# A one-token attention and MLP mix: the output row's second half summed in a second column group of the TensorE array, and three weight loads cut differently

## The chip, the cores and the metric

The kernel runs on one core of one Trainium2 chip. The metric is the device time of the slowest (here: the only) core, in microseconds (us). Several executions are timed for each kernel, and one more is profiled. The span that a profile or a run lists for its core is about 1.8 us shorter than the time of that execution in most cases and repeats more closely, so I use both, and say which.

## The reference, cut to what matters

One token `x` (576 numbers) goes through two branches that are mixed by a gate: attention with 32 query heads over the last 4096 positions of a cache with 16 key/value heads, and a GELU MLP with 4608 hidden units.

```python
g = sigmoid((x * gate_w).sum(-1))
q = x @ wq                                   # 576 -> 32 heads x 128
o = softmax(q @ k.T / sqrt(128)) @ v         # last 4096 positions, 16 kv heads
a = o.reshape(4096) @ wo                     # 4096 -> 576
h = gelu(x @ w1 + b1)                        # 576 -> 4608
b = h @ w2 + b2                              # 4608 -> 576
y = g * a + (1 - g) * b
```

With one token there is almost no reuse: 53.6 MB of weights and cache are read, each byte is used once or twice, and every product is a matrix times one vector.

## The kernel before

All large transfers are issued in one queue in the order of use: w1, wq, eight K tiles, eight V tiles (with the first half of w2 among them), wo, and the second half of w2. The output row y is accumulated in PSUM (the memory that the matmuls write to) over the whole kernel. Its 576 fp32 columns are kept in two accumulators of 288, so each row of wo or w2 costs two matmuls with one stationary column:

```python
NH = D // 2                                            # 288
ya_ps = ps_y.tile([1, NH], FP32, name="ya_ps")
yb_ps = ps_y.tile([1, NH], FP32, name="yb_ps")

def y_add(vec, row, start=False, stop=False):
    nc.tensor.matmul(ya_ps[:], lhsT=vec, rhs=row[:, 0:NH], start=start, stop=stop, skip_group_check=True)
    nc.tensor.matmul(yb_ps[:], lhsT=vec, rhs=row[:, NH:D], start=start, stop=stop, skip_group_check=True)
```

The loads that the change touches, and the end of the kernel:

```python
for k in range(KM):                                    # KM = 4: w1 in four pieces
    nc.sync.dma_start(out=w1_m[:, k, :], in_=w1_src[:, k, :])
# ... (wq, K, softmax, V, first half of w2 cut)
for r in range(0, RO, 8):                              # RO = 32: wo in four pieces of 8 rows
    nc.sync.dma_start(out=wo_t[:, r : r + 8, :], in_=wo_src[:, r : r + 8, :])
for b, j0, j1 in [(1, 0, 9), (1, 9, 13), (1, 13, 16), (1, 16, NJ)]:   # NJ = 18 rows of w2
    load_w2(b, j0, j1)
# ... (scaling of o cut)
for r in range(RO):
    y_add(ov[:, r : r + 1], wo_t[:, r, :])
y_w2(1)                                                # 18 rows, y_add each

out_row = const.tile([1, D], BF16, name="out_row")
nc.vector.tensor_copy(out=out_row[:, 0:NH], in_=ya_ps[:])
nc.scalar.copy(out=out_row[:, NH:D], in_=yb_ps[:])
nc.sync.dma_start(out=out.rearrange("a b d -> (a b) d"), in_=out_row[:])
```

A "row" below is one `r` of wo or one `j` of w2: 128 partitions of 576 bf16 numbers, 147 KB, and two matmuls.

Of the kernel before, what the change touches and what calls it, by code (L numbers as in the profile page):

```python
# [8 lines left out]
FP32 = mybir.dt.float32  # L9
# [7 lines left out]
def kernel(  # L17
# [15 lines left out]
    nc = tc.nc  # L33

    P = 128
    D = 576
# [7 lines left out]
    NJ = FB // P  # L44
    NF = NB * NJ
    NPAIR = Hkv // 2
    KM = 4
# [9 lines left out]
    ps_y = ctx.enter_context(tc.tile_pool(name="ps_y", bufs=1, space=bass.MemoryType.PSUM))  # L57
# [15 lines left out]
    w1_m = w1_t[:, 0 : KM * F].rearrange("p (k n) -> p k n", k=KM)  # L73
    w1_l = w1_t[:, KM * F :]
    w1_src = B_w1[0:DM, :].rearrange("(p k) n -> p k n", k=KM)
    for k in range(KM):
        nc.sync.dma_start(out=w1_m[:, k, :], in_=w1_src[:, k, :])
    nc.sync.dma_start(out=w1_l, in_=B_w1[DM:D, :].rearrange("r (two n) -> (r two) n", two=2))

    wq_t = big.tile([P, KM * Hq * Dh + QH], BF16, name="wq_t", tag="A")  # L80
# [43 lines left out]
    for j in range(4):  # L124
        nc.vector.tensor_copy(
            out=perm[:, j], in_=idv[:, j // 2, :, j % 2].unsqueeze(1).to_broadcast([P, 4, 32])
# [9 lines left out]
    for t in range(2):  # L136
# [3 lines left out]
        lhsT=xd[:].rearrange("p a t -> p (a t)"),  # L140
        rhs=one_b[0:1, 0:2],
        start=True,
        stop=True,
# [9 lines left out]
        out=junk_row[:],  # L153
# [17 lines left out]
        out=omg[:], in0=g_t[:], scalar1=-1.0, scalar2=1.0, op0=ALU.mult, op1=ALU.add  # L171
# [3 lines left out]
        out=b2g[:], in0=b2_row[:], scalar1=omg[0:1, 0:1], scalar2=None, op0=ALU.mult  # L175
# [2 lines left out]

    NH = D // 2
    ya_ps = ps_y.tile([1, NH], FP32, name="ya_ps")  # L180
    yb_ps = ps_y.tile([1, NH], FP32, name="yb_ps")

    def y_add(vec, row, start=False, stop=False):
        nc.tensor.matmul(ya_ps[:], lhsT=vec, rhs=row[:, 0:NH], start=start, stop=stop, skip_group_check=True)  # L184
        nc.tensor.matmul(yb_ps[:], lhsT=vec, rhs=row[:, NH:D], start=start, stop=stop, skip_group_check=True)  # L185

    y_add(one_f[0:1, 0:1], b2g[0:1, :], start=True)


    h_ps = ps_s.tile([P, NF], FP32, name="h_ps", tag="s")  # L190
    for k in range(KM):
        for c in range(NF):
# [3 lines left out]
                lhsT=w1_m[:, k, f0 : (c // NJ + 1) * FB : NJ],  # L196
                rhs=xt[:, k : k + 1],
                start=(k == 0 and c == 0),
                stop=False,
                skip_group_check=True,  # L200
            )
    for j in range(NJ):
        nc.tensor.matmul(  # L203
            h_ps[:, j:NF:NJ],
            lhsT=w1_l[:, j:FB:NJ],
            rhs=xl[:, 0:2],
            start=False,
            stop=(j == NJ - 1),
            skip_group_check=True,
# [4 lines left out]
        out=hx[:], in0=h_ps[:], in1=b1_t[:].rearrange("p b j -> p (b j)"), op=ALU.add  # L214
# [4 lines left out]
        out=z2[:], in0=z2[:], scalar1=2.0 * C0 * 0.044715, scalar2=2.0 * C0, op0=ALU.mult, op1=ALU.add  # L219
# [8 lines left out]
        out=gt[:], in0=hx[:], scalar=omg[:, 0:1], in1=e_h[:], op0=ALU.mult, op1=ALU.mult  # L228
# [4 lines left out]
    for k in range(KM):  # L233
        for j in range(Hq):
            nc.tensor.matmul(  # L235
                q_ps[:, j : j + 1],
                lhsT=wq_m[:, k, j * Dh : (j + 1) * Dh],
                rhs=xt[:, k : k + 1],
                start=(k == 0 and j == 0),
                stop=False,  # L240
                skip_group_check=True,
            )
    for j in range(Hq // 2):
        nc.tensor.matmul(
            q_ps[:, j : Hq : Hq // 2],
            lhsT=wq_l[:, j * Dh : (j + 1) * Dh],
            rhs=xl[:, 0:2],
            start=False,
            stop=(j == Hq // 2 - 1),
            skip_group_check=True,  # L250
# [4 lines left out]
    for j in range(4):  # L255
        nc.tensor.matmul(
            qj_ps[:, j, :, :].rearrange("p i x -> p (i x)"),
            lhsT=perm[:, j, :, :].rearrange("p b l -> p (b l)"),
            rhs=q_b[:],
            start=True,  # L260
            stop=True,
        )
    for b in range(4):
# [4 lines left out]
            out=diag[:, :, 0:512].rearrange("p i (j m) -> p i j m", m=P)[:, :, :, 0:4],  # L268
            in_=qj_ps[rows].rearrange("p j i x -> p i j x"),
# [13 lines left out]
    for n in range(4):  # L283
        for e in range(2):
            nc.tensor.matmul(  # L285
                s_ps[:, n // 2, n % 2],
                lhsT=no_l[0:1, e, :],
                rhs=no_r[0:1, e, :],
                start=(e == 0),
                stop=False,  # L290
                skip_group_check=True,
            )
    for i in range(NPAIR):
        k_t = load_pair(A_k_cache, i)
        for c1 in range(2):
            kt = early[:, c1 * W : (c1 + 1) * W]
            nc.vector.transpose(  # L297
                out=kt.bitcast(FP32), in_=k_t[:, c1 * W : (c1 + 1) * W].bitcast(FP32)
            )
            kv = kt.rearrange("p (n c b k t) -> p n c b k t", n=2, b=2, k=32, t=2)  # L300
            for j in range(4):
                for n in range(2):
                    nc.tensor.matmul(  # L303
                        s_ps[:, c1, n],
                        lhsT=qz[:, i, j, :],
                        rhs=kv[:, n, :, j // 2, :, j % 2],
                        start=False,
                        stop=(i == NPAIR - 1 and j == 3),
                        skip_group_check=True,
# [4 lines left out]
    for c1 in range(2):  # L314
        nc.vector.reduce_max(
            out=m2[:, c1 : c1 + 1], in_=s_ps[:, c1].rearrange("p n k -> p (n k)"), axis=AX.X
# [19 lines left out]
    for c1 in range(2):  # L336
        nc.scalar.activation(  # L337
            out=p_x[:, c1 * 1024 : (c1 + 1) * 1024],
            in_=s_ps[:, c1].rearrange("p n k -> p (n k)"),
# [6 lines left out]
            out=pt[:, c1 * NCH : (c1 + 1) * NCH, :].rearrange("p c h -> p (c h)"),  # L346
            in_=p_x[:, c1 * 1024 : (c1 + 1) * 1024],
# [3 lines left out]
    for c1 in range(2):  # L351
        nc.vector.tensor_scalar(
            out=sl[:, c1, :], in0=lo32[:], scalar1=sums[:, c1 : c1 + 1], scalar2=None, op0=ALU.mult
# [8 lines left out]
    for a in range(4):  # L362
        nc.vector.tensor_scalar(
            out=rh[:, :, a], in0=rg[:], scalar1=hi4[:, a : a + 1], scalar2=None, op0=ALU.mult
# [7 lines left out]
    def load_w2(b, j0, j1):  # L372
        nc.sync.dma_start(out=w2_t[:, b, j0:j1, :], in_=w2_src[:, b, j0:j1, :])

    def y_w2(b, j0=0, j1=NJ):
        for j in range(j0, j1):
            y_add(gt[:, b * NJ + j : b * NJ + j + 1], w2_t[:, b, j, :], stop=(b == NB - 1 and j == NJ - 1))

    for i in range(NPAIR):
# [3 lines left out]
        for c in range(2 * NCH):  # L383
            nc.tensor.matmul(  # L384
                o_ps[:, 4 * i : 4 * i + 4],
                lhsT=v_t[:, c, :],
                rhs=pt[:, c, 4 * i : 4 * i + 4],
                start=(c == 0),
                stop=(c == 2 * NCH - 1),
# [6 lines left out]
    RO = Hq * Dh // P  # L396
    wo_t = big.tile([P, RO, D], BF16, name="wo_t", tag="A")
    wo_src = A_wo.rearrange("(p r) n -> p r n", r=RO)
    for r in range(0, RO, 8):
        nc.sync.dma_start(out=wo_t[:, r : r + 8, :], in_=wo_src[:, r : r + 8, :])  # L400
    for b, j0, j1 in [(1, 0, 9), (1, 9, 13), (1, 13, 16), (1, 16, NJ)]:
        load_w2(b, j0, j1)


# [2 lines left out]
        out=om[:], in0=o_ps[:].unsqueeze(2).to_broadcast([P, Hq, 4]), in1=rh[:], op=ALU.mult  # L407
# [8 lines left out]
    for r in range(RO):  # L416
        y_add(ov[:, r : r + 1], wo_t[:, r, :])
    y_w2(1)

    out_row = const.tile([1, D], BF16, name="out_row")  # L420
    nc.vector.tensor_copy(out=out_row[:, 0:NH], in_=ya_ps[:])  # L421
    nc.scalar.copy(out=out_row[:, NH:D], in_=yb_ps[:])  # L422
    nc.sync.dma_start(out=out.rearrange("a b d -> (a b) d"), in_=out_row[:])


# [28 lines left out]
```

## Time and profile before

| | before |
|---|---|
| time, median of the runs | 136.38 us at first (3 runs), 136.42 with the runs added later (6) |
| span of the profiled execution | 134.6 us |
| bytes read | 53.6 MB |
| last byte of w2 landed | 130.63 us |
| y's last matmul ended | 132.06 us |

The first view is the page's strip: the span in 40 equal slices of 3.4 us, busy time in tenths for TensorE (PE), the granted TensorE clock in tenths (PEclk), the DMA engines, and what they moved.

```profile
PE   1289989570499798979679219799752253798692
PEclk9999999999999999999999975557975555569999
DMA  4999999999999999999999999999999999999940
GB/s 121 417 424 428 421 443 414 427 420 429 429 429 424 424 433 419 433 414 443 414 443 407 438 425 446 400 438 409 438 414 429 424 411 424 416 416 427 401 170 0
```

The DMA engines never stop from the second slice to the 38th. The transfers set the time, and only the first 2 us and what comes after the last byte can be anything else. So the end is what matters. The next view is the timeline of TensorE there (start, duration, engine, line, operation, output and inputs, shape; in brackets how long the engine was idle and who ended it).

```profile
127.47 0.28 PE L184 MATMUL ya_ps<-w_t,gt 128*1 128x288 bf16 x1 [1.04 <-DMA w_t<-in_B_w_dram]
127.59 0.28 PE L185 MATMUL yb_ps<-w_t,gt 128*1 128x288 bf16 x1
127.71 0.28 PE L184 MATMUL ya_ps<-w_t,gt 128*1 128x288 bf16 x1
...
131.75 0.29 PE L185 MATMUL yb_ps<-w_t,gt 128*1 128x288 bf16 x1
```

L184 is the first half of y, L185 the second. From 127.47, when w2's piece of 9 rows has landed, the 36 matmuls of w2's 18 rows start one every 122 ns without a gap; 0.28 is the length that the profile gives to one. The trace's semaphore records say when each of the 16 DMA engines finished its share of a piece: w2's last four pieces were complete at 127.43, 128.86, 129.90 and 130.63 us. TensorE did not wait for the last three of them: it was behind, and ended 1.43 us after the last byte. The chain of waits (start, duration, what) says the same: it goes from matmul to matmul and not to a transfer.

```profile
131.92 0.14 PE yb_ps L185
132.05 0.02 issue
132.08 0.39 ACT out_row L422
```

### The profile page before, as it was taken

Reading aid. Unit: us, or ns where it says so; the run is one execution under the profiler, and the core shown is the slowest. Engines: PE = TensorE matmul, PEld = TensorE weight load, DVE = VectorE, ACT = ScalarE, POOL = GpSimd, SP = SyncE. Lnnn points to the kernel's source line nnn. Section 1 sums busy time; section 2 is a strip of 40 time slices with the busy share of each in tenths; the row PEclk is TensorE's granted clock in tenths of the full one; section 3 lists DMA queues with packets and bytes.
Section 4 is the critical chain, followed back from the end, with each engine's and each line's share of the span. In section 5 each row is a group of like instructions: output and inputs, shape, how many; then the busy total and the mean of one; then the engine's idle time right before and its main releaser. Section 6 shows DMA issues by size and latency. Waiting matters only on the chain.

```text
span 134.6 us, 2438 instructions
## 1 busy us (share of the span) xinstructions
PE 92.4 (69%) x1116; PEld 57.9 (43%) x1116; DVE 50.3 (37%) x65; ACT 6.8 (5%) x11; POOL 2.8 (2%) x13
## 2 busy tenths in 40 slices
PE   1289989570499798979679219799752253798692
PEld 0285983470133233323233018765652253455461
DVE  2242013012958999998984845200000000100001
ACT  3600000001000000000000060000000000000001
POOL 8000000000000000000000000000000000000000
PEclk9999999999999999999999975557975555569999
DMA  4999999999999999999999999999999999999940
GB/s 121 417 424 428 421 443 414 427 420 429 429 429 424 424 433 419 433 414 443 414 443 407 438 425 446 400 438 409 438 414 429 424 411 424 416 416 427 401 170 0
DMA packets 5041, 53.76 MB, mean 400 GB/s; under 512 B 804, under 2 KB 808, under 8 KB 1448
## 3 DMA queue, kind: packets, MB, share of 16 engines
q1 hardware_dynamic: 4754, 53.61, 94.8%
q8 instruction: 8, 0.13, 0.4%
q10 hardware_dynamic: 278, 0.01, 0.1%
q14 instruction: 1, 0.01, 0.0%
HBM read 53.62 MB, written 0.00 MB: 398 GB/s over the span
## 4 chain that ended last, share of the span: by engine, by line
DMA 69%; PE 14%; DVE 6%; issue 5%; SPq 3%; ACTq 1%; ACT 0%; DVEq 0%
DMA w_t<-in_B_w_dram 36%; DMA kv_t<-in_A_k_cache_dram 26%; DMA b_t<-in_B_b_dram 8%; DVE early L297 6%; PE s_ps L303 5%; PE ya_ps L184 4%; PE yb_ps L185 4%; SPq L400 2%; PE o_ps L384 1%; SPq L276 1%; ACTq L63 0%; ACT out_row L422 0%; ACTq L67 0%; ACTq L65 0%; DVEq L297 0%
## 5 line engine op out<-in xcount | busy, mean ns | idle before, releaser
L303 PE MATMUL s_ps<-early 128*128 128x512 bf16 x128 | 32.9, 404 | 11.3 <-DVE early L297 11.3
L297 DVE STREAM_TRANSPOSE early<-kv_t 128x2048 f32<-128x2048 f32 x16 | 35.8, 2286 | 5.4 <-DMA kv_t<-in_A_k_cache_dram 3.4
L303 PEld LDWEIGHTS <-early 128*128 128x128 bf16 x128 | 12.9, 100 | 30.9 <-issue 17.4
L384 PE MATMUL o_ps<-pt,kv_t 128*128 128x4 bf16 x512 | 15.0, 166 | 14.5 <-DMA kv_t<-in_A_v_cache_dram 10.8
L384 PEld LDWEIGHTS <-kv_t 128*128 128x128 bf16 x512 | 14.7, 103 | 15.2 <-DMA kv_t<-in_A_v_cache_dram 11.1
L194 PE MATMUL h_ps<-xt,w_t 128*128 128x1 bf16 x144 | 9.6, 201 | 3.6 <-DMA w_t<-in_B_w_dram 3.6
L406 DVE TENSOR_TENSOR om<-o_ps,rh 128x128 bf16<-128x128 f32 x1 | 0.3, 292 | 30.1 <-PE o_ps L384 30.1
L184 PE MATMUL ya_ps<-w_t,gt 128*1 128x288 bf16 x36 | 10.6, 324 | 1.4 <-DMA w_t<-in_B_w_dram 1.4
L194 PEld LDWEIGHTS <-w_t 128*128 128x128 bf16 x144 | 9.3, 162 | 4.7 <-DMA w_t<-in_B_w_dram 3.7
L185 PE MATMUL yb_ps<-w_t,gt 128*1 128x288 bf16 x36 | 10.5, 322 | 0.0
L184 PE MATMUL ya_ps<-wo_t,ov 128*1 128x288 bf16 x32 | 9.6, 328 | 0.7 <-DMA wo_t<-in_A_wo_dram 0.7
L185 PE MATMUL yb_ps<-wo_t,ov 128*1 128x288 bf16 x32 | 9.5, 326 | 0.0
L421 DVE CAST out_row<-ya_ps 1x288 bf16<-1x288 f32 x1 | 0.4, 446 | 16.1 <-PE ya_ps L184 16.1
L235 PE MATMUL q_ps<-xt,wq_t 128*128 128x1 bf16 x128 | 3.7, 165 | 1.8 <-DMA wq_t<-in_A_wq_dram 1.8
L185 PEld LDWEIGHTS <-gt 128*1 128x1 bf16 x36 | 3.4, 94 | 3.5 <-issue 1.6
L235 PEld LDWEIGHTS <-wq_t 128*128 128x128 bf16 x128 | 3.6, 104 | 2.7 <-DMA wq_t<-in_A_wq_dram 1.9
L337 ACT ACTIVATE early<-s_ps,negm 128x1024 bf16<-128x1024 f32 x2 | 2.2, 1108 | 47.2 <-DVE negm L332 47.2
L184 PEld LDWEIGHTS <-gt 128*1 128x1 bf16 x36 | 3.4, 94 | 2.0
L185 PEld LDWEIGHTS <-ov 128*1 128x1 bf16 x32 | 3.0, 95 | 2.4 <-issue 0.6
L184 PEld LDWEIGHTS <-ov 128*1 128x1 bf16 x32 | 3.0, 95 | 2.2 <-DVE ov L414 0.4
L285 PE MATMUL s_ps<-no_r,no_l 1*128 1x512 bf16 x8 | 3.6, 620 | 0.4 <-DVE hx L213 0.4
L213 DVE TENSOR_TENSOR hx<-h_ps,b_t 128x36 f32<-128x36 f32 x1 | 0.2, 196 | 8.1 <-PE h_ps L203 8.1
(78 smaller groups left out, 36.2 us busy)
## 6 DMA issues: line engine op xcount, KB each, us to landing
kv_t<-in_A_k_cache_dram SPq DMA_DIRECT2D x8, 2048.0 KB, 25.1
kv_t<-in_A_v_cache_dram SPq DMA_DIRECT2D x8, 2048.0 KB, 14.9
w_t<-in_B_w_dram SPq DMA_DIRECT2D x4, 1152.0 KB, 10.1
wo_t<-in_A_wo_dram SPq DMA_DIRECT2D x4, 1152.0 KB, 21.8
wq_t<-in_A_wq_dram SPq DMA_DIRECT2D x2, 2048.0 KB, 16.1
w_t<-in_B_w_dram SPq DMA_DIRECT2D x1, 2592.0 KB, 20.7
w_t<-in_B_w_dram SPq DMA_DIRECT2D x1, 1296.0 KB, 27.2
w_t<-in_B_w_dram SPq DMA_DIRECT2D x2, 576.0 KB
```

Source lines behind the costliest of these rows:

```text
L184: nc.tensor.matmul(ya_ps[:], lhsT=vec, rhs=row[:, 0:NH], start=start, stop=stop, skip_group_check=True)
L185: nc.tensor.matmul(yb_ps[:], lhsT=vec, rhs=row[:, NH:D], start=start, stop=stop, skip_group_check=True)
L194: nc.tensor.matmul(h_ps[:, c : c + 1], lhsT=w1_m[:, k, f0 : (c // NJ + 1) * FB : NJ], rhs=xt[:, k : k + 1], start=(k == 0 and c == 0), sto ...
L235: nc.tensor.matmul(q_ps[:, j : j + 1], lhsT=wq_m[:, k, j * Dh : (j + 1) * Dh], rhs=xt[:, k : k + 1], start=(k == 0 and j == 0), stop=False ...
L276: nc.sync.dma_start(out=t[:], in_=cache[0, 2 * i : 2 * i + 2, Sk - W : Sk, :].rearrange("h (p c) d -> p h (c d)", p=64),)
L285: nc.tensor.matmul(s_ps[:, n // 2, n % 2], lhsT=no_l[0:1, e, :], rhs=no_r[0:1, e, :], start=(e == 0), stop=False, skip_group_check=True,)
L297: nc.vector.transpose(out=kt.bitcast(FP32), in_=k_t[:, c1 * W : (c1 + 1) * W].bitcast(FP32))
L303: nc.tensor.matmul(s_ps[:, c1, n], lhsT=qz[:, i, j, :], rhs=kv[:, n, :, j // 2, :, j % 2], start=False, stop=(i == NPAIR - 1 and j == 3), ...
L337: nc.scalar.activation(out=p_x[:, c1 * 1024 : (c1 + 1) * 1024], in_=s_ps[:, c1].rearrange("p n k -> p (n k)"), func=ACT.Exp, bias=negm[:, ...
L384: nc.tensor.matmul(o_ps[:, 4 * i : 4 * i + 4], lhsT=v_t[:, c, :], rhs=pt[:, c, 4 * i : 4 * i + 4], start=(c == 0), stop=(c == 2 * NCH - 1),)
L400: nc.sync.dma_start(out=wo_t[:, r : r + 8, :], in_=wo_src[:, r : r + 8, :])
L421: nc.vector.tensor_copy(out=out_row[:, 0:NH], in_=ya_ps[:])
```

## The change

The second half of y is accumulated at PSUM partition 32 instead of 0. The idea (the prediction below names its source) is that its matmuls then use another group of 32 columns of the array than those of the first half and can run beside them. wo comes in two pieces instead of four, w1 in three instead of four, and the second half of w2 in five instead of four, the last of one row.

```diff
-    for k in range(KM):
-        nc.sync.dma_start(out=w1_m[:, k, :], in_=w1_src[:, k, :])
+    for k0, k1 in [(0, 1), (1, 3), (3, KM)]:
+        nc.sync.dma_start(out=w1_m[:, k0:k1, :], in_=w1_src[:, k0:k1, :])
...
-    yb_ps = ps_y.tile([1, NH], FP32, name="yb_ps")
+    yb_t = ps_y.tile([33, NH], FP32, name="yb_t")
+    yb_ps = yb_t[32:33, :]
...
-    for r in range(0, RO, 8):
-        nc.sync.dma_start(out=wo_t[:, r : r + 8, :], in_=wo_src[:, r : r + 8, :])
-    for b, j0, j1 in [(1, 0, 9), (1, 9, 13), (1, 13, 16), (1, 16, NJ)]:
+    for r in range(0, RO, 16):
+        nc.sync.dma_start(out=wo_t[:, r : r + 16, :], in_=wo_src[:, r : r + 16, :])
+    for b, j0, j1 in [(1, 0, 7), (1, 7, 12), (1, 12, 15), (1, 15, 17), (1, 17, NJ)]:
         load_w2(b, j0, j1)
```

(`yb_ps[:]` becomes `yb_ps` in its three uses.)

More of the change, by code (lines that the diff above doesn't have):

```diff
@@ L180 @@
     ya_ps = ps_y.tile([1, NH], FP32, name="ya_ps")
-    yb_ps = ps_y.tile([1, NH], FP32, name="yb_ps")
+    yb_t = ps_y.tile([33, NH], FP32, name="yb_t")
+    yb_ps = yb_t[32:33, :]
     def y_add(vec, row, start=False, stop=False):
         nc.tensor.matmul(ya_ps[:], lhsT=vec, rhs=row[:, 0:NH], start=start, stop=stop, skip_group_check=True)
-        nc.tensor.matmul(yb_ps[:], lhsT=vec, rhs=row[:, NH:D], start=start, stop=stop, skip_group_check=True)
+        nc.tensor.matmul(yb_ps, lhsT=vec, rhs=row[:, NH:D], start=start, stop=stop, skip_group_check=True)
     y_add(one_f[0:1, 0:1], b2g[0:1, :], start=True)
@@ L421 @@
     nc.vector.tensor_copy(out=out_row[:, 0:NH], in_=ya_ps[:])
-    nc.scalar.copy(out=out_row[:, NH:D], in_=yb_ps[:])
+    nc.scalar.copy(out=out_row[:, NH:D], in_=yb_ps)
     nc.sync.dma_start(out=out.rearrange("a b d -> (a b) d"), in_=out_row[:])
```

## The prediction

> **What bounds the kernel now.** Transfers. The page's strip of 40 slices has the DMA engines at 9 tenths from slice 1 through 37, about 420 GB/s, for 53.6 MB. TensorE is busy 69%. Only the two ends are not transfer time. At the end (timeline, and the semaphore records of the trace): wo's four pieces land at 115.9, 118.7, 121.5 and 124.3 us, w2's last four at 127.4, 128.9, 129.9 and 130.63. From 127.47 TensorE runs 36 matmuls of y without a gap, one per 122 ns (18 pairs, 244 ns each), and ends at 132.06. So it ends 1.43 us after the last byte: here TensorE is the limit, by a little. Copy, issue and flight of the output follow: 2.5 us, to 134.6.
>
> **What the change does.**
>
> 1. *Column groups.* The first half's sum stays at PSUM partition 0, the second goes to partition 32. The Trainium skill, "TensorE: Matmul & The Clock Gate", section "Part 3: Packing small matmuls", says that matmuls with few output rows run concurrently when their outputs lie in different 32-partition groups. No run here shows it yet; before, the halves start 122 ns apart, in turn. The 4-column matmuls on V take 28 ns each, weight load included, so issuing is no obstacle. I expect a pair per 122 to 130 ns in place of 244.
>
> 2. *w2's end in five.* After the last landing only one pair is left, not two; with step 1, TensorE is waiting for each piece, and ends about 0.3 us after the last landing.
>
> 3. *wo in two, w1 in three.* Packets grow from 9,216 to 18,432 bytes. Mean packet times in the trace give 25.7 GB/s per DMA engine at 9,216 bytes and 26.5 at 16,384 or 20,736. My estimate from these is up to 0.5 us less for wo and half of w1, and 0.1 us more for w2's smaller packets: 0.3 us net.
>
> 4. *A cost:* wo's first matmul starts at about 118.5, not 115.9, and TensorE idles about 1.6 us between wo's halves. The granted clock was 0.5 at 100 to 119.9 us and rose 4.0 us after y's matmuls began. It may now rise as late as 127 to 130 us. At half clock 16 pairs take 3.9 us. Even so, 34 pairs from 124 us end between 130.6 and 131.5; without step 1 they would end at 132 to 134.
>
> **On the critical path:** 132.06 becomes 130.3 + 0.3 = 130.6, plus up to 0.3 for a late clock: 1.2 to 1.5 us saved of 136.38. Steps 1 and 2 are 1.1 of it, packets 0.3.
>
> **Predicted: 135.0 us, range 134.4 to 136.0.** Faster by over 2%: 0.03; within: 0.94; slower: 0.03.
>
> **What would show it.** Step 1: the timeline has the two halves starting within some 10 ns, pairs 125 ns apart when warm. Step 2: TensorE waits for w2 several times after 126 us, and the chain of waits ends with w2's last transfer and one pair. Step 3: w2's last landing at 130.2 to 130.5. Step 4: the clock's row of the strip lower in slices 35 to 38.
>
> **What would make it wrong.** The halves don't overlap (then 136.5 to 138, as wo's coarser pieces have spent the slack); the clock stays low to the end; small last packets or lagging DMA engines (half of them finish 1.8 us after the others now) move the last landing.

## The result, and the profile after

The changed kernel took 135.42 us (median of 6 runs, 135.28 to 135.71) against 136.42 (136.31 to 136.55) for the one before. The ratio is 0.9929, with a 95% interval of 0.9916 to 0.9941. Ratios here are the mean time of one kernel's fast runs over that of the other's in the same rounds, so they are not quite the ratio of the medians. 1.0 us was saved. This counts as "same" at 2%, but it is well outside the noise.

The strip of the changed kernel:

```profile
PE   1168989570398898778769326899451451454891
PEclk9999999999999999999999955555955555558689
DMA  4999999999999999999999999999999999999960
```

The transfers are as dense as before. TensorE's clock row has changed at the end: 5s and an 8-6-8-9 where there was a row of 9s. The timeline of TensorE at the end, at two places:

```profile
118.54 0.40 PE L186 MATMUL ya_ps<-wo_t,ov 128*1 128x288 bf16 x1 [3.03 <-DMA wo_t<-in_A_wo_dram]
118.55 0.40 PE L187 MATMUL yb_t<-wo_t,ov 128*1 128x288 bf16 x1
118.74 0.44 PE L186 MATMUL ya_ps<-wo_t,ov 128*1 128x288 bf16 x1
118.74 0.44 PE L187 MATMUL yb_t<-wo_t,ov 128*1 128x288 bf16 x1
...
130.31 0.28 PE L186 MATMUL ya_ps<-w_t,gt 128*1 128x288 bf16 x1 [0.25 <-DMA w_t<-in_B_w_dram]
130.31 0.28 PE L187 MATMUL yb_t<-w_t,gt 128*1 128x288 bf16 x1
130.43 0.28 PE L186 MATMUL ya_ps<-w_t,gt 128*1 128x288 bf16 x1
130.43 0.28 PE L187 MATMUL yb_t<-w_t,gt 128*1 128x288 bf16 x1
130.61 0.28 PE L186 MATMUL ya_ps<-w_t,gt 128*1 128x288 bf16 x1
...
```

The halves L186 and L187 now start within 10 ns of each other. So the column groups do run side by side, as the Trainium skill says in "TensorE: Matmul & The Clock Gate", Part 3. But look at the distances. At 118.7 us the clock is at half, and from there on pairs are 240 ns apart (the next starts at 118.98); at 130.3 it is full, and they are 122 ns apart. A pair side by side at half clock takes as long as a pair in turn at full clock did (244 ns). TensorE waits for the piece before the last (0.25 us), so it has caught up, and its last pair starts at 130.61, 0.04 us after the last landing. In the chain of waits, a transfer now stands directly before the last three rows:

```profile
103.21 27.05 DMA w_t<-in_B_w_dram
130.26 0.04 issue
130.31 0.28 PE ya_ps L186
...
130.72 0.18 PE ya_ps L186
130.89 0.05 PE yb_t L187
130.94 0.43 DVE out_row L423
```

The pieces of w2 landed at 126.64, 128.43, 129.48, 130.26 and 130.57 us. The last landing has hardly moved (130.63 before). y's end moved from 132.06 to 130.94, by 1.12 us, of which 0.91 us reached the span (134.57 to 133.67). What comes after y's end takes 2.73 instead of 2.51 us. Some 0.07 of this is plain from the timelines: the two halves now finish together, so the 0.45 us copy of the first half no longer starts ahead of the second half's end, and the output is issued 0.50 instead of 0.43 us after y's end. The rest comes after the issue: from the output's landing to the end of the program it is 1.09 us instead of 0.95, in all three profiled kernels with wo in two pieces. The trace's records of SyncE show where it goes. The program ends with five semaphore waits of SyncE, one after the other. In the kernel before, two of them were over when the output landed and three came after it; in the changed kernel all five came after it, 62 to 69 ns apart. How many come after goes with the number of transfers that the kernel issues: 36 (wo in two) leave five, 38 three, 39 (e2, e6) two and 40 (e11) one, and the time from landing to end is 1.09, 0.95, 0.89 and 0.83 us.

### The profile page after: what moved, and what is told of

It is laid out like the page before. It is cut to its first block, busy times and chain, and to the rows that moved or that the text cites. A ratio compares the mean times of both kernels' runs of the same rounds, so it can differ in the third digit from the quotient of the medians.

```text
span 133.7 us, 2436 instructions
## 1 busy us (share of the span) xinstructions
PE 83.9 (63%) x1116; PEld 52.5 (39%) x1116; DVE 50.2 (38%) x65; ACT 6.9 (5%) x11; POOL 2.8 (2%) x13
## 4 chain that ended last, share of the span: by engine, by line
DMA 68%; DVE 13%; PE 8%; issue 7%; ACT 1%; ACTq 1%; DVEq 0%
DMA kv_t<-in_A_k_cache_dram 31%; DMA w_t<-in_B_w_dram 20%; DMA kv_t<-in_A_v_cache_dram 13%; DVE early L299 9%; DMA b_row<-in_B_b_dram 4%; PE s_ps L305 4%; PE o_ps L386 2%; DVE pt L347 2%; DVE m_660 L317 2%; ACT early L339 1%; PE t_ps L359 1%; PE ya_ps L186 0%; PE mb_ps L330 0%; ACTq L63 0%; PE mt_ps L322 0%
## 5 line engine op out<-in xcount | busy, mean ns | idle before, releaser
L305 PE MATMUL s_ps<-early 128*128 128x512 bf16 x128 | 32.0, 394 | 12.4 <-DVE early L299 12.4
L186 PE MATMUL ya_ps<-wo_t,ov 128*1 128x288 bf16 x32 | 7.1, 405 | 5.3 <-DMA wo_t<-in_A_wo_dram 5.3
L186 PE MATMUL ya_ps<-w_t,gt 128*1 128x288 bf16 x36 | 7.4, 368 | 0.3 <-DMA w_t<-in_B_w_dram 0.2
L187 PE MATMUL yb_t<-w_t,gt 128*1 128x288 bf16 x36 | 7.4, 370 | 0.0
L187 PE MATMUL yb_t<-wo_t,ov 128*1 128x288 bf16 x32 | 7.1, 405 | 0.0
L187 PEld LDWEIGHTS <-ov 128*1 128x1 bf16 x32 | 3.5, 113 | 5.2 <-issue 5.2
L186 PEld LDWEIGHTS <-ov 128*1 128x1 bf16 x32 | 3.6, 113 | 3.1 <-DVE ov L416 0.4
L186 PEld LDWEIGHTS <-gt 128*1 128x1 bf16 x36 | 3.7, 105 | 2.6
L187 PEld LDWEIGHTS <-gt 128*1 128x1 bf16 x36 | 3.6, 106 | 0.8 <-issue 0.7
```

The lines of the kernel that those rows point to most:

```text
L187: nc.tensor.matmul(yb_ps, lhsT=vec, rhs=row[:, NH:D], start=start, stop=stop, skip_group_check=True)
L305: nc.tensor.matmul(s_ps[:, c1, n], lhsT=qz[:, i, j, :], rhs=kv[:, n, :, j // 2, :, j % 2], start=False, stop=(i == NPAIR - 1 and j == 3), ...
```

## The experiments

The theory with which I went into the experiments was the prediction's: the column groups bring nearly all of the gain. The rival was that the cut of the transfers does. Each alone turned out to bring more than half of it, since both remove the same backlog, and the clock is why the groups alone bring no more. This table has all runs but the one with a different purpose (e7); "span" is the median of the spans that the runs list (4 to 11 runs each), and "landed" (the last piece of w2) and "y's end" (by the chain of waits) are of the profiled execution, in us.

| kernel | groups | w1 / wo / w2's end | ratio | span | landed | y's end |
|---|---|---|---|---|---|---|
| before | no | 4 / 4 / four | 1 | 134.7 | 130.63 | 132.06 |
| e1_groups | yes | 4 / 4 / four | 0.9973 | 134.1 | 130.61 | 131.96 |
| e2_groups_w2five | yes | 4 / 4 / five | 0.9950 | 133.8 | 131.02 | 131.39 |
| e4_wo_four | yes | 3 / 4 / five | 0.9932 | 133.7 | 130.78 | 131.15 |
| changed kernel (e12) | yes | 3 / 2 / five | 0.9907 (0.9929 at first) | 133.65 | 130.60 | 130.98 |
| e3_pieces_only | no | 3 / 2 / five | 1.0134 | 136.05 | 130.61 | 133.89 |
| e6_w2five_only | no | 4 / 4 / five | 0.9948 | 134.0 | 130.67 | 131.41 |
| e11_w2six_no_groups | no | 4 / 4 / six | 0.9927 | 133.9 | 130.89 | 131.49 |
| e9_groups_by_halves | yes, wo by halves | 4 / 4 / four | 0.9914 | 133.8 | 130.66 | 131.15 |
| e10_wo_four_by_halves | yes, wo by halves | 3 / 4 / five | 0.9911 | 133.6 | 130.68 | 131.06 |
| e5_groups_wo_junk | yes, extra matmuls | 4 / 4 / four | 1.0044 | 135.5 | 132.19 | 132.68 |
| e8_wo_four_junk | yes, extra matmuls | 3 / 4 / five | 1.0029 | 135.0 | 132.06 | 132.43 |

The last four experiments (e9 to e12) shared a set of rounds in which some executions of the kernel before took up to 137.9 us while their spans stayed at 134.5 to 134.8. This makes their ratios a little too good and their intervals wide (0.9870 to 0.9944 for e12). Compare those four with each other, and by span with the rest. Where a ratio and a span seem to disagree (0.9914 and 133.8 for e9, 0.9950 and 133.8 for e2), the span is the better witness.

### e1_groups: the column groups alone

```diff
--- before
-    yb_ps = ps_y.tile([1, NH], FP32, name="yb_ps")
+    yb_t = ps_y.tile([33, NH], FP32, name="yb_t")
+    yb_ps = yb_t[32:33, :]
```

> The kernel before with the second half's sum at PSUM partition 32, and nothing else. My theory: this one edit is nearly the whole gain, because at the end TensorE was 1.43 us behind the last landing and catches up when pairs take 122 ns. I expect the last landing unchanged at 130.6 us, y's last matmul ending near 131.0 instead of 132.06, a wait for data before w2's last piece, and 0.9 to 1.0 us saved (ratio 0.993, a time near 135.5 us). Rival: the gain comes from the larger and differently cut transfers; then this run stays within 0.2 us of before (ratio 0.999 to 1.000).

Measured: 135.96 us (135.69 to 136.99), ratio 0.9973 with an interval of 0.9947 to 0.9998. Between the two expectations, so my theory missed: the groups alone bring about half of the change's gain. The profiled execution, the longest of this kernel's spans (134.5; the others 133.7 to 134.2), shows how they can bring nothing at all. The timeline's last rows:

```profile
131.22 0.44 PE L185 MATMUL ya_ps<-w_t,gt 128*1 128x288 bf16 x1
131.23 0.45 PE L186 MATMUL yb_t<-w_t,gt 128*1 128x288 bf16 x1
131.47 0.44 PE L185 MATMUL ya_ps<-w_t,gt 128*1 128x288 bf16 x1
131.47 0.45 PE L186 MATMUL yb_t<-w_t,gt 128*1 128x288 bf16 x1
```

The halves overlap, and yet the pairs are 240 ns apart to the very end. The clock is at half. The next view gives, for stretches of the span, TensorE's busy time and the granted clock (the number after POOL's busy time; then the DMA share and GB/s). I chose the stretches so that each is one interval of the clock's own: in every trace the recorded clock is either 0.5 or 1.0, and lasts 3.41 us or a multiple of it (but for the last interval, which the end of the record cuts; the first record is at about 40 us, so the 9s of the strips before that rest on no record). This is the free-running window of 3413 ns of the Trainium skill ("TensorE: Matmul & The Clock Gate", Part 1), and here the trace agrees to the digit. First the kernel before, then e1_groups:

```profile
116.50:119.90 3.40, 3.40 (x16) 1.79 (x14) 0.00 (x0) 0.00 (x0) 0.00 (x0) 0.50 1.02 417
119.90:123.30 3.40, 3.40 (x30) 2.31 (x28) 0.00 (x0) 0.00 (x0) 0.00 (x0) 0.99 1.01 421
...
```

```profile
118.60:122.00 3.40, 2.62 (x22) 1.32 (x23) 0.00 (x0) 0.00 (x0) 0.00 (x0) 0.50 1.00 418
122.00:125.40 3.40, 2.68 (x24) 1.28 (x22) 0.00 (x0) 0.00 (x0) 0.00 (x0) 0.50 1.02 424
...
```

Before, TensorE was busy for all of the first window (3.40 of 3.40 us), because 8 rows in turn at half clock take 3.8 us and the next piece of wo was there before they were done. The clock rose, and stayed up. With the groups, 8 rows take 1.9 us of the 2.8 us between two landings, the windows from 118.6 to 128.9 us are 77, 79 and 69% busy, and the clock does not rise until 132.3 us, when all is over. A new theory follows: **running the halves side by side shortens TensorE's busy time, this keeps the clock at half, and a pair then costs what it cost before.** How bad it is probably differs from execution to execution, because the window is not tied to the kernel's start; this fits that the spans of e1_groups spread over 0.8 us and those of the kernel before over 0.3. e5 and e9 test it.

### e2_groups_w2five: and w2's end in five

```diff
--- e1_groups
-    for b, j0, j1 in [(1, 0, 9), (1, 9, 13), (1, 13, 16), (1, 16, NJ)]:
+    for b, j0, j1 in [(1, 0, 7), (1, 7, 12), (1, 12, 15), (1, 15, 17), (1, 17, NJ)]:
```

> The run before it plus w2's end in five pieces. My theory: one pair instead of two is left after the last landing, so 0.1 us less than with the groups alone (ratio 0.992 to 0.993), and the landing no earlier, rather 0.05 to 0.1 us later, as the smaller packets cost a little. Rival (the cut of the transfers is what counts): at least 0.3 us less than with the groups alone.

Measured: 135.64 us (135.49 to 136.66), ratio 0.9950 (0.9927 to 0.9974); the span is 0.3 us shorter than that of e1_groups. The intervals of the two ratios overlap, so the 0.3 us is not sharp. It is the rival's number, and it fits the new theory: at half clock 9 rows take 2.2 us and are not done when the next 4 land 1.4 us later, while 7, 5, 3, 2 and 1 leave a smaller backlog. y ended 0.37 us after the last landing, against 1.35 in e1_groups.

### e3_pieces_only: all the cuts and no groups

```diff
--- changed kernel
-    yb_t = ps_y.tile([33, NH], FP32, name="yb_t")
-    yb_ps = yb_t[32:33, :]
+    yb_ps = ps_y.tile([1, NH], FP32, name="yb_ps")
```

> The changed kernel with both sums at partition 0 again: wo in two, w1 in three, w2's end in five, and no second column group. My theory: slower than before, because wo's first matmul waits until 118.5 us, TensorE idles between wo's halves, and then 34 pairs of 244 ns or more follow from 124.2 us: y ends at 132.5 us if the clock is up, up to 134 if it is not; 136.9 to 138.3 us (ratio 1.003 to 1.014). Rival (the transfers are what counts): faster than before by 0.5 us or more (ratio 0.996 or less).

Measured: 138.30 us (137.43 to 139.14), ratio 1.0134 (1.0100 to 1.0167). As the theory had it. The pieces landed as early as in the changed kernel (the last at 130.61), and TensorE was 3.3 us behind; the chain's end is matmul after matmul:

```profile
133.63 0.12 PE ya_ps L184
133.75 0.14 PE yb_ps L185
133.89 0.02 issue
133.91 0.39 ACT out_row L422
```

With wo in two pieces TensorE idles from 115.6 to 118.6 us, and then has 50 rows to do. In turn that cannot be made up. So the groups are worth 2.4 us of span in the company of wo in two pieces. But that is a loss which wo in two pieces brought about.

### e4_wo_four: wo in four again

```diff
--- changed kernel
-    for r in range(0, RO, 16):
-        nc.sync.dma_start(out=wo_t[:, r : r + 16, :], in_=wo_src[:, r : r + 16, :])
+    for r in range(0, RO, 8):
+        nc.sync.dma_start(out=wo_t[:, r : r + 8, :], in_=wo_src[:, r : r + 8, :])
```

> The changed kernel with wo in four pieces again (groups, w1 in three and w2's end in five stay). My theory: wo's cut is worth nothing either way once the groups are there, since TensorE catches up before the last landing in both: 135.3 to 135.5 us (ratio 0.992 to 0.993), with y's matmuls on wo from 115.9 us and the clock up by about 120 us. If packets of 18,432 bytes were faster than those of 9,216, as my prediction had it, this would be 0.4 us slower than the changed kernel (ratio 0.996).

Measured: 135.59 us (135.44 to 135.63), ratio 0.9932 (0.9920 to 0.9944), where the changed kernel had 0.9929 in its own rounds. Wo's cut is worth nothing that these times can show, as expected, and so are the larger packets, on which the prediction put 0.3 us. In its profile the clock was up from 120.8 to 124.2 us and again from 127.6 us.

### e5_groups_wo_junk: the groups alone, with TensorE kept busy

```diff
--- e1_groups
+    jk = ps_s.tile([1, NH], FP32, name="jk", tag="s")
     for r in range(RO):
         y_add(ov[:, r : r + 1], wo_t[:, r, :])
+        nc.tensor.matmul(jk[:], lhsT=ov[:, r : r + 1], rhs=wo_t[:, r, 0:NH], start=True, stop=True)
```

> The groups alone, as in e1_groups, and one more matmul of 288 columns for each of wo's 32 rows, whose result nobody reads: it keeps TensorE as busy through wo as it was before. Theory: e1_groups saved only half of what was expected because pairs that run side by side halve TensorE's busy time, the granted clock stays at 0.5 to the end, and a pair then costs 240 ns, as much as before. So more work makes this faster: clock 1.0 from about 120 to beyond 128 us, pairs on w2 122 ns apart, y ending at 131.0 to 131.2 us in place of 131.9, and 135.4 to 135.6 us (ratio 0.992 to 0.994, e1_groups 0.9973). Rival (something else costs in the groups): the 32 extra matmuls make no difference or a slower kernel, 136.0 us or more.

Measured: 137.28 us (136.97 to 137.30), ratio 1.0044 (1.0030 to 1.0058). By the time, a clear miss. The trace shows that the clock did what the theory says, and that something else was lost. The stretches:

```profile
119.00:121.00 2.00, 2.00 (x16) 1.05 (x14) 0.00 (x0) 0.00 (x0) 0.00 (x0) 0.50 1.03 429
121.00:124.00 3.00, 3.00 (x38) 2.08 (x37) 0.00 (x0) 0.00 (x0) 0.00 (x0) 0.99 1.01 422
```

And the timeline:

```profile
128.50 0.29 PE L185 MATMUL ya_ps<-w_t,gt 128*1 128x288 bf16 x1
128.51 0.29 PE L186 MATMUL yb_t<-w_t,gt 128*1 128x288 bf16 x1
130.42 0.28 PE L185 MATMUL ya_ps<-w_t,gt 128*1 128x288 bf16 x1 [1.63 <-DMA w_t<-in_B_w_dram]
```

The clock rose at 121.0, w2's first nine pairs took 122 ns each, and TensorE then waited 1.63 us for w2's second piece. That piece came late: its shares finished between 126.95 and 130.38 us, against 126.83 to 128.83 in e1_groups, and the last piece was complete only at 132.19. The page's section on DMA queues points to the cause. First e1_groups, then e5_groups_wo_junk (packets, MB, share of the engines):

```profile
q8 instruction: 8, 0.13, 0.4%
```

```profile
q8 instruction: 9, 0.15, 0.4%
```

Instructions come over the same DMA engines, in packets of 16,384 bytes. The 64 extra instructions brought a ninth such fetch before the end, at 128.2 us by the trace's packet records. It took 1.03 us, in the middle of the last pieces, and in each piece after it one of the 16 shares comes 1.4 to 1.5 us after all the others (for the last piece 132.19 and 130.68). The Trainium skill ("Runtime: NRT & Kernel Launch", section "Instruction fetch mechanics") describes fetches in 16 KiB blocks of 256 instructions and calls their cost mostly hidden. The size agrees. Whether TensorE itself waits for fetches I did not look into; but in a kernel that waits for the DMA engines the cost is not hidden: one engine got late, and the span rose by 1.4 us over e1_groups.

### e9_groups_by_halves: the same question without extra instructions

```diff
--- e1_groups
-    for r in range(RO):
-        y_add(ov[:, r : r + 1], wo_t[:, r, :])
+    for r0 in range(0, RO, 8):
+        for y, n0 in ((ya_ps[:], 0), (yb_ps, NH)):
+            for r in range(r0, r0 + 8):
+                nc.tensor.matmul(y, lhsT=ov[:, r : r + 1], rhs=wo_t[:, r, n0 : n0 + NH],
+                                 start=False, stop=False, skip_group_check=True)
```

The same matmuls, so ordered that neighbours in wo's part share a column group and run in turn. w2's rows still run in pairs.

> The groups alone (e1_groups), but wo's rows are taken eight at a time, all first halves and then all second halves: the same matmuls and no more instructions, but no two neighbours in different groups, so wo keeps TensorE busy as long as before; w2's pairs still run side by side. A cleaner form of e5_groups_wo_junk, whose 64 extra instructions brought a ninth 16 KB instruction fetch at 128 us that made one DMA engine 1.6 us later. Theory (the clock ate half of the groups' gain): clock 1.0 from about 120 us, no ninth fetch before the end, last landing 130.6, w2's pairs 122 ns apart, y ending at 131.0 to 131.2 us, 135.4 to 135.6 us (ratio 0.992 to 0.994). Rival (it was not the clock): as e1_groups, 0.997 or more.

Measured: 135.73 us (135.53 to 136.12), ratio 0.9914 (0.9881 to 0.9948); span 133.8, against 134.1 for e1_groups, and 133.7 against 134.5 in the two profiled executions. No ninth fetch. The stretches, again cut at the clock's own windows:

```profile
115.30:118.80 3.50, 3.06 (x18) 1.64 (x19) 0.24 (x2) 0.00 (x0) 0.00 (x0) 0.51 1.01 415
...
125.60:129.00 3.40, 1.69 (x23) 0.88 (x22) 0.00 (x0) 0.00 (x0) 0.00 (x0) 1.00 0.93 374
```

TensorE is busy 87% of the first stretch, the clock rises after it, and stays up although the next two are only 66% busy and the last one shown 50%. w2's pairs then take 122 ns, TensorE waits for every piece, and the chain ends in a transfer and two rows, with y's end at 131.15 us, inside what was expected:

```profile
113.12 17.53 DMA w_t<-in_B_w_dram
130.66 0.04 issue
130.70 0.28 PE ya_ps L185
```

So taking the overlap away where there was time to spare made the overlap pay where there was none. This supports the clock theory. The size is 0.8 us between the two profiled executions, but only about 0.3 us between the medians of the spans, since e1_groups is not always as unlucky as in its profile.

### e6_w2five_only: one of the cuts and nothing else

```diff
--- before
-    for b, j0, j1 in [(1, 0, 9), (1, 9, 13), (1, 13, 16), (1, 16, NJ)]:
+    for b, j0, j1 in [(1, 0, 7), (1, 7, 12), (1, 12, 15), (1, 15, 17), (1, 17, NJ)]:
```

> The kernel before with w2's end in five pieces, and nothing else: no second column group. Theory: the first piece is 7 rows instead of 9 and lands 0.7 us earlier; TensorE at the full clock, which waited 1.04 us for it before, goes on from there without a gap, so y ends at 131.1 to 131.4 us instead of 132.06 and 0.6 to 0.9 us are saved (ratio 0.9935 to 0.9955): about as much as the groups bring. Rival, the prediction's own reading (the groups are what counts, the fifth piece is 0.1 us): ratio 0.998 or more.

Measured: 135.84 us (135.66 to 136.20), ratio 0.9948 (0.9934 to 0.9962). As the theory had it, and against the prediction's reading. The timeline shows where it comes from:

```profile
126.20 0.29 PE L185 MATMUL yb_ps<-wo_t,ov 128*1 128x288 bf16 x1
126.79 0.28 PE L184 MATMUL ya_ps<-w_t,gt 128*1 128x288 bf16 x1 [0.30 <-DMA w_t<-in_B_w_dram]
```

The wait in front of w2 is 0.30 us instead of 1.04. TensorE starts the same 36 matmuls 0.68 us earlier and ends 0.65 us earlier. The first piece, not the last, was what had to be made smaller.

### e11_w2six_no_groups: six pieces, no groups

```diff
--- before
-    for b, j0, j1 in [(1, 0, 9), (1, 9, 13), (1, 13, 16), (1, 16, NJ)]:
+    for b, j0, j1 in [(1, 0, 5), (1, 5, 10), (1, 10, 13), (1, 13, 15), (1, 15, 17), (1, 17, NJ)]:
```

> The kernel before with w2's end in six pieces of 5, 5, 3, 2, 2 and 1 rows and no second column group. Theory: what counts is how much work is left when the last byte lands, and the cut alone can bring that down: TensorE goes on from wo's end at 126.2 without a wait, one row is left after the last landing at 130.6, y ends at 131.0 to 131.2 us, 135.4 to 135.7 us (ratio 0.992 to 0.995), as good as the changed kernel within 0.2 us. Rival (the groups are needed for the whole gain): at or above w2's five pieces without groups, 0.9948 or more.

Measured: 135.69 us (135.66 to 137.11), ratio 0.9927 (0.9884 to 0.9969); the changed kernel in the same rounds 135.61. The spans are 133.9 and 133.65, so within about 0.25 us of the changed kernel, and 0.8 of its 1.05 us, without any column group. Part of this is the end of the program, which takes 0.12 us less than before in e11 and 0.14 us more in the changed kernel; y's end itself came 0.57 us earlier than before, and 1.08 us in e12. y ended 0.60 us after the last landing (TensorE was still a row or two behind, in turn), later than I had expected (131.49 instead of 131.2 at most), and the last landing was later too (130.89).

### e10_wo_four_by_halves and e12_after_again: is anything left?

e10 is e4_wo_four with wo's rows ordered as in e9; e12 is the changed kernel, unedited.

> e4_wo_four (groups, w1 in three, wo in four, w2's end in five) with wo's rows by halves, so that the clock is up when w2 comes. e4_wo_four ended y within 0.35 us of its last landing at half clock, so there is little left: 135.3 to 135.5 us (ratio 0.991 to 0.993), the same as the changed kernel within 0.2 us, and less spread between runs. A gain of 0.3 us or more over the changed kernel would say that TensorE still held it up.

> The changed kernel, unedited, in the same rounds as the other three, so that differences of 0.1 to 0.3 us can be read: 135.4 us (ratio 0.9929 as measured before, 0.992 to 0.994).

Measured: e10 135.55 us (135.40 to 136.57; ratio 0.9911), e12 135.61 us (135.40 to 136.04; ratio 0.9907), spans 133.6 and 133.65. They are the same within the noise. No version that I ran beats the changed kernel clearly. In e12's profile the clock was at half from 97.3 to 128.0 us without a break, and in the first profile it was up once in between (121.2 to 124.6); y ended at 130.98 and 130.94. So the clock's earlier course no longer shows. But the clock still matters there. When it rose at 128.0 us in e12, TensorE had just finished wo's rows and was 1.3 us behind the landing of w2's first piece (126.69); at 240 ns each, w2's 18 rows would have ended at about 132.4 us (an estimate from these numbers), not at 130.98. What brought the clock up in time is that wo's second half gives TensorE 16 rows at once: at half clock they keep it busy for 3.8 us, so that the window from 124.6 to 128.0 us was busy throughout in both profiles. After that a row takes 122 ns, and the rows land about 350 ns apart (two rows 0.73 to 0.78 us).

The expectation of e10 errs on one point: e4_wo_four did not end y at half clock, its clock was up from 127.6 us on.

### e8_wo_four_junk: the extra matmuls again

e4_wo_four with the `jk` matmul of e5.

> Groups, w1 in three, wo in four, w2's end in five (e4_wo_four), with the extra matmul for each of wo's rows. Theory: with the clock up and the small last pieces nothing of TensorE is left after the last landing but one pair; but e4_wo_four was already within 0.4 us of its last landing, so at most 0.1 to 0.2 us less than that one: 135.3 to 135.5 us (ratio 0.991 to 0.993). A larger gain (135.1 us or less) would say that TensorE still held up more than I read from the trace.

Measured: 136.83 us (136.81 to 137.14), ratio 1.0029 (1.0013 to 1.0044), a miss for the same reason as e5: a ninth instruction fetch at 128.4 us, and the last landing at 132.06. It repeats that finding with other cuts.

### e7_eight_engines: can the uneven finish of the DMA engines be used?

In the changed kernel the 16 shares of the last piece finished between 128.51 and 130.57 us: about half of the engines were done 2 us before the rest. The semaphore records show that the number of late shares grows through the kernel, from one at 22 us to about eight at 112 us, and the page counts 8 instruction fetches; I take the fetches for the cause, and e5 and e8 support it. If the early ones could take more, up to about 1 us would be won. I gave 16 of the 128 partitions to two transfers of 8 partitions each.

```diff
--- changed kernel
+    for p0 in (112, 120):
+        nc.sync.dma_start(out=w2_t[p0 : p0 + 8, 1, :, :], in_=w2_src[p0 : p0 + 8, 1, :, :])
     for b, j0, j1 in [(1, 0, 7), (1, 7, 12), (1, 12, 15), (1, 15, 17), (1, 17, NJ)]:
-        load_w2(b, j0, j1)
+        nc.sync.dma_start(out=w2_t[0:112, b, j0:j1, :], in_=w2_src[0:112, b, j0:j1, :])
```

> The changed kernel, but the rows of w2's second half for partitions 112 to 127 come in two transfers of 8 partitions each, and the five pieces have 112 partitions. If a transfer of 8 partitions goes over 8 of the 16 DMA engines, always the same, these 8 get two packets of 20,736 bytes more and the other 8 get less, a shift of 0.77 us each way. In the changed kernel about 8 engines finish 2.06 us after the others. If the 8 engines used are the early ones: the last landing goes from 130.57 to about 129.8 us and the time to 134.6 to 134.9 us. If they are the late ones: the last landing goes to 131.3 us and the time to 136.0 to 136.3 us. If the late engines are a mixture: the same or a little slower than the changed kernel. No theory of the change hangs on it; it asks whether the uneven finish of the DMA engines can be used.

Measured: 144.54 us (144.19 to 144.75), ratio 1.0581 (1.0563 to 1.0598). None of the three expectations holds. Stretches of this kernel:

```profile
118.00:122.00 4.00, 3.19 (x28) 1.79 (x29) 0.00 (x0) 0.00 (x0) 0.00 (x0) 0.50 1.01 401
122.00:126.00 4.00, 0.81 (x8) 0.28 (x5) 0.00 (x0) 0.00 (x0) 0.00 (x0) 0.90 1.02 146
...
130.00:134.00 4.00, 1.97 (x18) 0.92 (x13) 0.00 (x0) 0.00 (x0) 0.00 (x0) 0.50 0.98 231
```

From the first of these transfers on the engines are as busy as before and move 146 to 231 GB/s instead of 400 and more. Single packets got slower: one of 20,736 bytes took 2.04 us (median) instead of the 0.77 that such packets of w2's first half take elsewhere, and one of 8,064 bytes 0.62 instead of 0.31. So how the partitions are dealt out to the engines can cost a factor of two. Pieces of 112 partitions are slow by themselves: the last packet of the 8-partition transfers was over at 129.8 us, and the packets of 3,456 bytes, all begun after 130.7 us, took 246 ns (median) instead of 139 in the changed kernel. Whether transfers of 8 partitions slow the others down too, and why any of this is so, stays open, and so does the question that the run was meant for.

## Why the prediction was right or wrong, point by point

The time lay in the range (134.4 to 136.0; 135.42 measured), and "within 2%" was right. The saving was 1.0 us where I had 1.2 to 1.5.

- **What bounds the kernel:** right. The last landing stayed at 130.57 to 130.60 us (130.63 before), and nearly all of the gain came from what follows it.
- **Step 1, the halves side by side:** right as a mechanism. They start within 10 ns, and pairs are 122 ns apart at full clock.
- **Step 2, one row after the last landing, y's end 0.3 us after it:** right; 0.37 us in the changed kernel. The sign that was to show it came only in part: TensorE waited for w2 once by more than 0.1 us (0.25 us, for the piece before the last) and not several times, because it did wo's second half at half clock and was behind until about 129.3 us.
- **Step 3, larger packets, 0.3 us net: this is the step that failed, by its size.** I took mean packet times over all packets of a size (25.7 GB/s at 9,216 bytes, 26.5 above). The mean for 9,216 bytes holds w1's packets too, and with them the first packets of the kernel, which took up to 1.15 us at the start of everything. Summed per DMA engine, wo's packets took 11.31 us in four pieces and 11.08 in two, the same to 0.01 us in all eleven traces without extra matmuls or odd partitions: 0.23 us saved. For w1, three pieces cannot be told from four (11.64 to 11.88 us either way), and w2's smaller packets gave 0.10 us back, as predicted. That is 0.13 us in sum. The last landing moved by 0.06 us (0.03 in e12). It was 130.68 and 130.78 us in e10 and e4, which keep wo in four, but two traces with the same transfers (e2 and e6) differ by 0.35 us, so single landings do not settle a tenth.
- **Step 4, the later clock:** right in kind. wo's first matmul came at 118.54, and the clock rose at 121.2, fell at 124.6 and rose again at 128.0. It cost nothing that shows: y ended 0.37 us after the last landing, and 0.38 us in e10, where the clock was up from 119.6 us on. This rests on the second rise at 128.0 us (see e12).
- **"Steps 1 and 2 are 1.1 of it":** right as a sum for y's end (1.12 us), wrong as an account of the parts. I took step 2 for a detail worth the last row. In fact e6 shows that w2's cut alone brings 0.7 us of span and e1 that the groups alone bring 0.6, and together they bring 0.9 (e2) to 1.05: both remove the same 1.43 us of backlog, and neither can remove more than there is. I had also charged the clock's fall to wo's two pieces alone; e1 shows that the groups bring it about by themselves.
- **"Without step 1 TensorE would end at 132 to 134" and "136.5 to 138":** y's end at 133.89 us and a time of 138.30 us (e3): the first at the upper end, the second 0.3 us above it.
- **What I left out:** the end of the program, 0.22 us longer from y's last matmul on. With the last landing (130.3 predicted, 130.57 measured) this is the whole difference between 135.0 and 135.42, and a little more.

Not settled: how busy a window must be for the clock to rise (below), and e7's slow packets.

## What to carry to other kernels

When transfers set the time, only the work that is left when the last byte lands can be saved; compute when each piece lands and when its work is done, and make the first of the last pieces small enough that the engine never falls behind, before you speed up the engine. Work packed more densely on TensorE leaves it idle for longer, and in e1_groups a TensorE that was idle for a fifth to a third of each window was left at half the clock: if a stage is short on time, let the stage before it keep TensorE busy, by order rather than by extra instructions. In a kernel that keeps the DMA engines full, count instructions too: eight 16 KB fetches came with the first 2,060 or so of TensorE's here, about one for every 256, and each took about a microsecond of one DMA engine.

## What the Trainium skill lacked or had wrong

- "TensorE: Matmul & The Clock Gate", Parts 1 and 3: the page gives the packing's gain and the clock's rule apart, but not that packing works against the clock. e1_groups: pairs overlapped, the clock stayed at 0.5 from 94.7 to 132.3 us, and a pair cost 240 ns, as much as 244 for two in turn at full clock.
- The same page asks for about 3.4 us of sustained activity and names no busy share. Here the clock rose after windows with TensorE 76% busy (changed kernel, 117.7 to 121.2 us: 2.66 of 3.5), 87% (e9) and 100% (before), and did not rise after 77 and 79% (e1). Nor did it rise after a window that the profile counts as busy throughout, nearly all with 4-column matmuls on V (before, 82.4 to 85.8 us: 3.41 of 3.41, 97 of 100 matmuls). So the profile's busy share is not the measure itself; it can be used only between windows with the same matmuls, and even there the border is not sharp. It stayed up through a stretch that was 50% busy (e9) and fell after one that was 33% busy (changed kernel, 121.2 to 124.6).
- "Runtime: NRT & Kernel Launch", section "Instruction fetch mechanics": the cost of crossing a 16 KiB block is called mostly hidden. A fetch's packet took 1.0 to 1.1 us in these traces, and with one more of them before the end (9 instead of 8) the last landing came at 132.19 us in place of 130.61 (e5 and e1) and at 132.06 in place of 130.78 (e8 and e4).
- "DMA: Bandwidth & Descriptors" says how a transfer's partitions decide the number of engines, but not that pieces of 112 partitions, which still finish in 16 shares, can have packets nearly twice as slow: 3,456 bytes took 246 ns in them and 139 in pieces of 128 (e7 and the changed kernel).
